# Two-layer mixture-of-experts kernel after an attention layer on one Trainium2 core: transposes of the attention weights from TensorE to VectorE, scores one batch further ahead, and item lists computed along the free dimension

## The chip, the cores and the metric

The kernel runs on one core of a Trainium2 chip. The metric is the device time in microseconds (us) of one execution, the median of three runs. Engines are named as in the profile: PE is TensorE (matrix multiplication), DVE is VectorE, ACT is ScalarE, POOL is GpSimd, SP is SyncE, which here only issues DMAs.

## The reference

Three layers, all in fp32. First an attention in two steps, for 8 batches of 8 heads, with 32 packed queries `p` and 576 positions. Then two mixture-of-experts layers over the 4608 rows, each row to the expert with the largest logit; the second also skips rows.

```python
p_packed = sm_attn(p, k, v)              # 32 queries against 576 keys, per head
out = sm_attn(q, p_packed, p_packed)     # 576 queries against 32 packed rows
x = out.transpose(0, 2, 1, 3).reshape(8 * 576, 512)
# layer 1: e = argmax(x @ w_gate); x = gate * relu(x @ w1[e]) @ w2[e]
# layer 2: rows with x @ w_skip > 0 only:
#          e = argmax(x @ w_gate); x = x + gate * relu(x @ w1[e]) @ w2[e]
```

With the inputs given nearly all rows of a batch choose one expert in the first layer. The few others and the second layer are worked through as lists of items (batch, expert), found while the kernel runs.

## The kernel before

**Loop over batches.** The main loop runs over the 8 batches of the first layer. The main work of batch `b` is `gen_M`: for each half of the 576 columns, `stage1` (8 hidden tiles, line 750, each of 6 matmuls of 128x288) and `stage2` (4 output tiles, line 779, each of 24 matmuls). Every product is made from split operands (a high part and a low part `...l`), three matmuls for one. `stage1` ends in a high half on ACT (`hh`, line 762) and a low half on DVE (`hl`, line 763); `stage2` reads the eight `hh` and `hl` in the order 3, 2, 1, 0, 7, 6, 5, 4.

**What is woven in.** `Weave` goes through the 48 steps of the main work and lets side work (other generators) issue its instructions between them, each at a share of the loop that the `plan` and `sides` give. Side work marked `TE` may only come at every fourth step, so that different kinds of small matmuls stand together in one lump between the large ones. The side work of batch `b` is the attention of the next batches: `gen_S` of batch `b+1` and `b+2` (first softmax), `gen_T` of batch `b+1` (second softmax), `gen_R` (routing), `gen_pre` (weights of the next batch's expert), and the routing of the second layer. The order on each engine comes from this program order and a scheduler at build time. Every engine works through its own queue in order.

**gen_S** makes scores (32 heads' rows, line 384, `s<-kT,pT`), their maxima on DVE (line 426), exponentials on ACT into `a1` (line 438; 128 partitions, 2x576), and the sums. Then PE turns `a1` by 8 transposes of 128x128 (line 455) and one of the tail `tl` (line 459), ACT copies the results from PSUM to `aT` (line 458), and PE multiplies by `v` (lines 468 and 474). The result `pk` is scaled on DVE (line 483), turned on PE (line 488), and gives three small sums on DVE: `kb`, `kw`, `ks` (lines 493 to 501). `gen_T` needs `ks` for a matmul that picks the batch's expert (line 521); it stands in PE's queue right behind the score matmuls of `gen_T`.

**Lists.** `first_item` (end of batch 6) finds the first item of the second layer. `y_list` finds all others while the first item's main work runs (`e_item`, 32 steps of 12 matmuls). Both count flags over partitions by small matmuls with `sel`, `tri` and `ones` (lines 892, 896, 902, 917, 922, 923, 955). `x_flags` counts the left-over rows of the first layer (line 1020). The list `lyB` is read by SP, which then loads the next item's rows and weights.

Of the kernel before, what the change touches and what calls it, by code (L numbers as in the profile page):

```python
# [9 lines left out]
F32 = mybir.dt.float32  # L10
# [11 lines left out]
E = 8  # L22
# [6 lines left out]
XB = 6  # L29
# [89 lines left out]
def attn_moe_kernel(ctx, tc, q, k, v, p, wg, w11, w12, w21, w22, out):  # L119
# [48 lines left out]
    lyA = ct("lyA", [32, 1], I32)  # L168
# [19 lines left out]
    def gen_consts():  # L188
        for t, x in ((sel, 0.0), (valy, 0.0), (GMx, 0.0), (FM, 0.0), (FX, 0.0), (csx, 0.0)):
            nc.gpsimd.memset(t, x)  # L190
        nc.gpsimd.memset(sel[0:1, :], 1.0)
        nc.gpsimd.memset(valy[:, 3:4], 1.0)
# [27 lines left out]
        nc.vector.tensor_copy(valy[:, 0:1], q8[0:64, :])  # L220
        nc.vector.tensor_copy(valy[:, 2:3], m8[0:64, :])
# [16 lines left out]
    lnA = const.tile([64, 1], F32, name="lnA")  # L238
# [72 lines left out]
    def gen_prefix(fc, nch, n):  # L311
# [13 lines left out]
        nc.vector.tensor_copy(pc[:, 0:nch], p0[0:n, 0:nch])  # L325
        return pc
# [80 lines left out]
    def gen_S(b):  # L407
        d = st[b]
# [34 lines left out]
        tl = wk_p.tile([128, 2, 64], F32, name="tl")  # L443
        nc.vector.tensor_copy(tl, a1[:, :, 512:S])
# [6 lines left out]
        aT = wk_p.tile([128, 9, 128], F32, name="aT")  # L451
# [7 lines left out]
        nc.tensor.transpose(ats[2][:, 0:128], tl.rearrange("p x c -> p (x c)"), ident)  # L459
        nc.scalar.copy(out=aT[:, 8, :], in_=ats[2][:, 0:128])  # L460
# [157 lines left out]

    def gen_attn():
        for b in range(1, B):  # L620
            yield from gen_T(b)
            if b + 1 < B:
                if b == 1:
                    with tc.issue_after(hold[-1]):
                        load_all(b + 1)
                else:
# [242 lines left out]
    def y_flags(f2, v, k):  # L869
        nc.vector.tensor_scalar(out=f2[:, 0, :], in0=v, scalar1=float(SMALL), scalar2=None, op0=ALU.is_gt)  # L870
        if k > 1:
            nc.vector.scalar_tensor_tensor(
                out=f2[:, 1, :], in0=v, scalar=0.0, in1=f2[:, 0, :], op0=ALU.is_gt, op1=ALU.subtract
            )

    def first_item():
# [11 lines left out]
        f2 = rt.tile([32, 3, n], F32, name="f2", bufs=1)  # L888
        y_flags(f2, fl.rearrange("p b e -> p (b e)"), 1)
        yield  # L890
        ps = mt("f0")
        nc.tensor.matmul(out=ps[0:n, 0:1], lhsT=f2[:, 0, :], rhs=sel[:, 0:1], start=True, stop=True)
        fc = rt.tile([64, 3], F32, name="yfc", bufs=1)
        nc.vector.tensor_copy(fc[:, 0:1], ps[0:n, 0:1])
        yield
        nc.tensor.matmul(out=ps[0:n, 8:9], lhsT=tri[0:n, 0:n], rhs=fc[:, 0:1], start=True, stop=True)
        nc.vector.scalar_tensor_tensor(
            out=lnA, in0=ps[0:n, 8:9], scalar=1.0, in1=fc[:, 0:1], op0=ALU.is_equal, op1=ALU.mult
        )
        yield  # L900
        l0 = mt("l0")
        nc.tensor.matmul(out=l0[0:32, 0:1], lhsT=valy, rhs=lnA, start=True, stop=True)
        nc.vector.tensor_copy(lyA, l0[0:32, 0:1])
        yield

    def y_list():
# [856 lines left out]
```

## Time and profile before

| | |
|---|---|
| median of 3 runs | 584.71 us (584.62 to 585.27) |
| profiled execution, its own time | 585.04 us |
| its span, first to last instruction | 583.3 us |
| mean granted clock of TensorE | 0.998 |
| PE busy | 573.2 us (98%) |
| DVE busy | 327.9 us (56%) |
| ACT busy | 217.9 us (37%) |
| POOL busy | 132.2 us (23%) |

The span is 1.7 us shorter than the execution's own time. A busy time is the union of an engine's instructions, and matmuls are pipelined: the mean duration of one is longer than the distance between two starts.

### The profile page before, as it was taken

Reading aid. Unit: us, or ns where it says so; the run is one execution under the profiler, and the core shown is the slowest. Engines: PE = TensorE matmul, PEld = TensorE weight load, DVE = VectorE, ACT = ScalarE, POOL = GpSimd, SP = SyncE. Lnnn points to the kernel's source line nnn. Section 1 sums busy time; section 2 is a strip of 40 time slices with the busy share of each in tenths; the row PEclk is TensorE's granted clock in tenths of the full one; section 3 lists DMA queues with packets and bytes.
Section 4 is the critical chain, followed back from the end, with each engine's and each line's share of the span. In section 5 each row is a group of like instructions: output and inputs, shape, how many; then the busy total and the mean of one; then the engine's idle time right before and its main releaser. Section 6 shows DMA issues by size and latency. Waiting matters only on the chain. (4 is left out here: it accounts for less than half of the span.)

```text
span 583.3 us, 14454 instructions
## 1 busy us (share of the span) xinstructions
PE 573.2 (98%) x5798; PEld 532.2 (91%) x5799; DVE 327.9 (56%) x995; ACT 217.9 (37%) x477; POOL 132.2 (23%) x121
## 2 busy tenths in 40 slices
PE   8899999999999999999999999999999999999996
PEld 6489899899999989989989998899999999998796
DVE  3898658566566757646756864346736327162111
ACT  3464542452462353444346234133414325042110
POOL 3051331331240150133133114020301310130031
PEclk9999999999999999999999999999999999999999
DMA  8945978787485767826714616997047583731065
GB/s 338 364 163 202 420 324 318 262 312 269 156 302 167 308 209 238 330 74 261 277 58 187 236 45 223 330 302 265 6 173 255 99 342 93 199 97 70 1 90 86
DMA packets 33806, 123.23 MB, mean 211 GB/s; under 512 B 5424, under 2 KB 15536, under 8 KB 25648
## 3 DMA queue, kind: packets, MB, share of 16 engines
q1 hardware_dynamic: 28304, 116.16, 53.3%
q0 software_dynamic: 3824, 4.70, 6.2%
q10 hardware_dynamic: 1584, 1.18, 0.6%
q8 instruction: 51, 0.84, 0.6%
q14 instruction: 43, 0.35, 0.2%
HBM read 92.77 MB, written 29.26 MB: 209 GB/s over the span
## 5 line engine op out<-in xcount | busy, mean ns | idle before, releaser
L779 PE MATMUL y<-hh,W2h 128*128 128x288 f32 x512 | 154.4, 302 | 0.0
L779 PE MATMUL y<-hl,W2h 128*128 128x288 f32 x512 | 151.2, 295 | 0.0
L779 PE MATMUL y<-hh,W2l 128*128 128x288 f32 x512 | 150.9, 295 | 0.0
L779 PEld LDWEIGHTS y<-hh,W2h 128*128 128x128 f32 x512 | 96.0, 188 | 4.9 <-DVE Q1l L646 2.8
L779 PEld LDWEIGHTS y<-hh,W2l 128*128 128x128 f32 x512 | 96.4, 188 | 0.0
L779 PEld LDWEIGHTS y<-hl,W2h 128*128 128x128 f32 x512 | 96.2, 188 | 0.1
L646 POOL TENSOR_TENSOR W2l<-W2c,W2h 128x1024 fp32r<-128x1024 f32 x28 | 66.7, 2391 | 124.6 <-ACT W2h L644 105.5
L750 PE MATMUL h<-A2h,Q1h 128*128 128x288 f32 x256 | 76.6, 299 | 0.0
L750 PE MATMUL h<-A2h,Q1l 128*128 128x288 f32 x256 | 75.7, 296 | 0.0
L750 PE MATMUL h<-A2l,Q1h 128*128 128x288 f32 x256 | 75.5, 295 | 0.0
L763 DVE SCALAR_TENSOR_TENSOR hl<-h,hh 128x288 fp32r<-128x288 f32 x128 | 56.4, 452 | 29.5 <-ACT hh L762 29.4
L762 ACT ACTIVATE hh<-h 128x288 fp32r<-128x288 f32 x128 | 51.7, 412 | 55.3 <-PE h L750 52.8
L750 PE MATMUL h<-eXh,eW1h 128*128 128x288 f32 x192 | 57.7, 301 | 0.2 <-issue 0.2
L1380 PE MATMUL y<-ihh,iW2h 128*128 128x288 f32 x192 | 56.8, 296 | 0.0
L1380 PE MATMUL y<-ihl,iW2h 128*128 128x288 f32 x192 | 56.6, 295 | 0.0
L1380 PE MATMUL y<-ihh,iW2l 128*128 128x288 f32 x192 | 56.6, 295 | 0.0
L750 PE MATMUL h<-eXl,eW1h 128*128 128x288 f32 x192 | 56.5, 295 | 0.0
L750 PE MATMUL h<-eXh,eW1l 128*128 128x288 f32 x192 | 56.5, 294 | 0.0
L750 PEld LDWEIGHTS h<-A2h,Q1h 128*128 128x128 f32 x256 | 48.0, 187 | 2.1 <-DVE Q1l L646 0.8
L750 PEld LDWEIGHTS h<-A2h,Q1l 128*128 128x128 f32 x256 | 48.1, 188 | 0.2
L750 PEld LDWEIGHTS h<-A2l,Q1h 128*128 128x128 f32 x256 | 48.1, 188 | 0.0
L644 ACT CAST W2h<-W2c 128x1024 fp32r<-128x1024 f32 x30 | 31.6, 1054 | 39.3 <-PE y L779 21.8
(311 smaller groups left out, 937.3 us busy)
## 6 DMA issues: line engine op xcount, KB each, us to landing
eW<-in_w_dram SPq DMA_DIRECT2D x8, 2048.0 KB
W2c<-in_w_dram SPq DMA_DIRECT2D x30, 512.0 KB
v<-in_v_dram SPq DMA_DIRECT2D x7, 1280.0 KB
W1c<-in_w_dram SPq DMA_DIRECT2D x8, 1024.0 KB
y<-in_w_dram SPq DMA_DIRECT2D x8, 1024.0 KB
kT<-in_k_dram SPq DMA_DIRECT2D x7, 1152.0 KB
qT<-in_q_dram SPq DMA_DIRECT2D x7, 1152.0 KB
x2d<-y SPq DMA_DIRECT2D x7, 1152.0 KB
```

Of the source, the lines that this page charges most:

```text
L644: a = nc.scalar.copy(out=hi, in_=x)
L646: z = eng.tensor_tensor(out=lo, in0=x, in1=hi.bitcast(F32), op=ALU.subtract)
L750: m = nc.tensor.matmul(out=ps[:, 0:rh.shape[2]], lhsT=l[:, t, 128 * f:128 * f + 128], rhs=r[:, t, :], start=(n == 0), stop=(n == 3 * kt - 1),)
L762: us[0]["hh"] = nc.scalar.activation(out=hh[:, f, :], in_=ps[:, 0:n_], func=ACTF.Relu).ins
L763: ins = nc.vector.scalar_tensor_tensor(out=hl[:, f, :], in0=ps[:, 0:n_], scalar=0.0, in1=hh[:, f, :].bitcast(F32), op0=ALU.max, op1=ALU.su ...
L779: nc.tensor.matmul(out=ps[:, 0:HALF], lhsT=l[:, f, :], rhs=r[:, f, :], start=(n == 0), stop=(n == 23))
L1380: nc.tensor.matmul(out=ps[:, 0:HALF], lhsT=l[:, f, 128 * t:128 * t + 128], rhs=r[:, f, c], start=(n == 0), stop=(n == 23))
```

## The change

For batches 3 to 7 `a1` is no longer turned by PE. DVE does it in 32x32 blocks: 16 instructions (`gen_Sx`), each from 32 partitions of `a1` to 32 partitions of `aT`, 8 blocks (256 elements per partition) each. The tail keeps its PE transpose. For this, the scores and exponentials (`gen_Sa`) of a batch come one batch earlier, and its `k` and `p` with them; batch 3's scores go into the second half of batch 1 as a new piece of side work. Batches 0 to 2 are as before. `first_item` and `y_list` now hold the 64 flags in the free dimension on 32 partitions: a prefix sum in six DVE additions, a DVE transpose, and one product of two matmuls at the end take the place of the matmuls with `sel`, `tri` and `ones`. `x_count` moves the count of left-over rows into the matmul lump of the prefix, and a `yield TE` joins another small matmul to a later lump. The loads for the item behind the first come 0.03 of a loop later.

```diff
+    def gen_S(b):
+        yield from gen_Sa(b)
+        yield from gen_Sb(b)
...
+    def tail(b):
+        tl = st[b]["tl"] = wk_p.tile([128, 2, 64], F32, name="tl")
+        nc.vector.tensor_copy(tl, st[b]["a1"][:, :, 512:S])
+
+    def gen_Sx(b):
...
+        for h in range(4):
+            for g in range(4):
+                nc.vector.transpose(
+                    out=aT[32 * g:32 * g + 32, 0:8, 32 * h:32 * h + 32].rearrange("p (x j) c -> p x j c", x=2),
+                    in_=a1[32 * h:32 * h + 32, :, 0:512].rearrange("p x (j g c) -> p x j g c", g=4, c=32)[:, :, :, g, :],
+                )
+                if (h, g) == (3, 3):
+                    tail(b)
+                yield
...
-        ats = [mt("at") for _ in range(3)]
-        for x in range(2):
-            for j in range(4):
-                last = nc.tensor.transpose(ats[x][:, 128 * j:128 * j + 128], a1[:, x, 128 * j:128 * j + 128], ident).ins
-            if b == 0 and x == 0:
-                keep(3, last)
-            nc.scalar.copy(out=aT[:, 4 * x:4 * x + 4, :].rearrange("p j c -> p (j c)"), in_=ats[x])
+        if b < AHEAD:
...
+        else:
+            aT = d["aT"]
...
-                    load_all(b + 1)
-                yield from gen_S(b + 1)
+                    if b + 2 < B:
+                        load_k(b + 2)
+                    load_q(b + 1)
+                    load_v(b + 1)
+                    yield from gen_Sb(b + 1)
...
+        for i in range(6):
+            a, z, k = P[i % 2], P[1 - i % 2], 2 ** i
+            nc.vector.tensor_tensor(out=z[:, :, H:], in0=a[:, :, H:], in1=a[:, :, H - k:H + n - k], op=ALU.add)
...
-            nc.tensor.matmul(out=ps[0:n, i:i + 1], lhsT=f2[:, i, :], rhs=sel[:, 0:1], start=True, stop=True)
...
+        for k in range(2):
+            nc.tensor.matmul(out=l0[0:32, 0:2 * w + 3], lhsT=valy[:, k, :], rhs=O[:, k, :], start=(k == 0), stop=(k == 1))
...
+                    if b == 1:
...
+                        s3 = gen_Sa(3)
+                        sides.append((part(s3, 1), 1, 0.3, 0.35))
+                        sides.append((s3, 6, 0.405, 0.5, TE))
+                    sides.append((gen_Sx(b + 2), 17, *((0.55, 0.84) if b == 1 else (0.45, 0.82))))
+                    if b + 3 < B:
+                        s4 = gen_Sa(b + 3)
+                        sides.append((part(s4, 1), 1, 0.6, 0.65))
+                        sides.append((s4, 5, 0.81, 1.0, TE))
...
-        return [(part(ld, 1), 1, 0.37, 0.38), (ld, 1, 0.56, 0.57), (pre(), 8, 0.55, 1.0)]
+        return [(part(ld, 1), 1, 0.37 + z, 0.38 + z), (ld, 1, 0.56, 0.57), (pre(), 8, 0.55 + z, 1.0)]
```

How the instructions stand on an engine is given below in rows of the built program: line, operation, output and inputs, shape, and how many in a row.

DVE in the second half of the first `stage1` of batches 2 to 5, up to the sum `ks` for which PE's line 521 (570 in the changed kernel) waits. Before:

```order
L272 STREAM_TRANSPOSE gT<-GM_76 128x160
L763 SCALAR_TENSOR_TENSOR hl<-h,hh 128x288
L845 SCALAR_TENSOR_TENSOR fT<-gT,once 128x160
L763 SCALAR_TENSOR_TENSOR hl<-h,hh 128x288
L850 TENSOR_REDUCE csB<-fT 128x1
L763 SCALAR_TENSOR_TENSOR hl<-h,hh 128x288 x2
L493 TENSOR_REDUCE kb<-ps 128x4
L497 TENSOR_TENSOR kw<-wgAB,kb 128x32
L501 TENSOR_REDUCE ks<-kw 128x8
```

The same place in the changed kernel; the first of the four `hl` stands just ahead of these rows, and one more transpose `aT<-a` five rows ahead:

```order
L273 STREAM_TRANSPOSE gT<-GM_75 128x160
L818 SCALAR_TENSOR_TENSOR hl<-h,hh 128x288
L484 STREAM_TRANSPOSE aT<-a_3389 32x8x32
L818 SCALAR_TENSOR_TENSOR hl<-h,hh 128x288
L484 STREAM_TRANSPOSE aT<-a_3389 32x8x32
L818 SCALAR_TENSOR_TENSOR hl<-h,hh 128x288
L542 TENSOR_REDUCE kb<-ps 128x4
L484 STREAM_TRANSPOSE aT<-a_3389 32x8x32
L546 TENSOR_TENSOR kw<-wgAB,kb 128x32
L900 SCALAR_TENSOR_TENSOR fT<-gT,once 128x160
L550 TENSOR_REDUCE ks<-kw 128x8
```

Four transposes now stand ahead of `ks`, and `csB` has gone behind it.

DVE in the second half of batch 1, around the eight `hl` of the second `stage1`. Before:

```order
L570 STREAM_TRANSPOSE A_1430<-T_1377 128x288 x2
L646 TENSOR_TENSOR A2l<-A_1430,A2h 128x576
L797 TENSOR_TENSOR y_145<-y,gB 128x288
L763 SCALAR_TENSOR_TENSOR hl<-h,hh 128x288 x8
L646 TENSOR_TENSOR A2l<-A_1430,A2h 128x576
```

In the changed kernel, from behind `A2l` up to the second `hl`; the pattern of one transpose and one `hl` goes on to the eighth `hl`, with two transposes in one place:

```order
L469 TENSOR_SCALAR sm<-sm 128x1
L472 RECIPROCAL rc_1515<-sm 128x1
L852 TENSOR_TENSOR y_144<-y,gB 128x288
L469 TENSOR_SCALAR sm<-sm 128x1
L484 STREAM_TRANSPOSE aT<-a_1605 32x8x32
L472 RECIPROCAL rc_1515<-sm 128x1
L484 STREAM_TRANSPOSE aT<-a_1605 32x8x32
L818 SCALAR_TENSOR_TENSOR hl<-h,hh 128x288
L484 STREAM_TRANSPOSE aT<-a_1605 32x8x32
L818 SCALAR_TENSOR_TENSOR hl<-h,hh 128x288
```

Four maxima (line 448) and two small instructions (line 455) of batch 3's scores also stand ahead, between the transposes of `A` and `A2l`; ten transposes in all stand ahead of the eighth `hl`.

PE in `y_list`, in the first item of the second layer; `h` are main matmuls. Before (the matmul of line 955 follows nine main matmuls behind these rows):

```order
L917 MATMUL f_7259<-sel,f_7255 64x1 x3
L750 MATMUL h<-eXh,eW1h 128x288
L750 MATMUL h<-eXl,eW1h 128x288
L750 MATMUL h<-eXh,eW1l 128x288
L922 MATMUL f_7259<-yfc,tri 64x2
L923 MATMUL f_7259<-yfc,ones 64x1
```

The changed kernel has one lump there, 36 main matmuls later than line 955 stood before, counted from the item's start:

```order
L805 MATMUL h<-eXl,eW1h 128x288
L805 MATMUL h<-eXh,eW1l 128x288
L1017 MATMUL l_7369<-Oy,valy 32x133 x2
L805 MATMUL h<-eXh,eW1h 128x288
L805 MATMUL h<-eXl,eW1h 128x288
```

Three lumps (917, 922 with 923, and 955) have become one, with two products of half the depth.

## Rows read from the trace of the kernel before

**Rows 1.** The page's busy times, and the longest wait of PE: total, times, longest.

```profile
PE 573.2 (98%) x5798; PEld 532.2 (91%) x5799; DVE 327.9 (56%) x995; ACT 217.9 (37%) x477; POOL 132.2 (23%) x121
...
PE keep L347 <- DVE fl L884: 1.7, 1, 1.7
```

**Rows 2.** PE's timeline, main matmuls in batch 1: start, duration, instruction.

```profile
100.03 0.30 PE L750 MATMUL h<-A2h,Q1l 128*128 128x288 f32 x1
...
104.96 0.29 PE L779 MATMUL y<-hh,W2h 128*128 128x288 f32 x1
```

**Rows 3.** PE's timeline, the transposes of batch 3's weights, in batch 2.

```profile
123.99 1.04 PE L455 MATMUL at<-ident,a 128*128 128x128 f32 x8
124.87 0.27 PE L459 MATMUL at<-ident,tl 128*128 128x128 f32 x1
```

**Rows 4.** Busy times over the loops of batches 2 to 5 (four windows).

```profile
sum 183.00, PE 182.86 PEld 171.64 DVE 113.75 ACT 77.71 POOL 47.10; mean PE 45.72 PEld 42.91 DVE 28.44 ACT 19.43 POOL 11.78
```

**Rows 5.** DVE's groups by shape: transposes, two copies, maxima; busy, mean ns.

```profile
L570 DVE STREAM_TRANSPOSE A<-T 128x288 f32<-128x288 f32 x32 | 13.5, 459 | 7.6 <-POOL T L566 7.6
L426 DVE TENSOR_REDUCE mx<-s 128x1 f32<-128x288 f32 x32 | 13.1, 447 | 6.5 <-PE s L384 6.5
L281 DVE STREAM_TRANSPOSE LT<-L 128x160 f32<-128x160 f32 x16 | 5.5, 346 | 10.4 <-PE L L825 10.4
L1261 DVE COPY xro<-xT 128x256 f32<-128x256 f32 x1 | 0.4, 424 | 0.9 <-PE xT L1260 0.9
L1100 DVE COPY xh<-hT 128x256 f32<-128x256 f32 x1 | 0.4, 415 | 0.0
L281 DVE STREAM_TRANSPOSE LT<-L 32x32 f32<-32x32 f32 x1 | 0.2, 205 | 0.9 <-PE L L1118 0.9
```

**Rows 6.** Timeline of DVE up to `ks`, and PE's matmul on it, batch 3.

```profile
177.00 0.34 DVE L272 STREAM_TRANSPOSE gT<-GM 128x160 f32<-128x160 f32 x1
177.27 0.16 DVE L266 TENSOR_TENSOR GM<-oh,g 128x40 f32<-128x40 f32 x1
...
178.81 0.30 DVE L850 TENSOR_REDUCE csB<-fT 128x1 f32<-128x160 f32 x1
179.03 0.81 DVE L763 SCALAR_TENSOR_TENSOR hl<-h,hh 128x288 fp32r<-128x288 f32 x2
179.76 0.28 DVE L493 TENSOR_REDUCE kb<-ps 128x4 f32<-128x128 f32 x1
180.31 0.21 DVE L501 TENSOR_REDUCE ks<-kw 128x8 f32<-128x32 f32 x1
...
181.57 0.17 PE L521 MATMUL s<-ks,ones 64*32 64x8 f32 x1
```

**Rows 7.** Timeline in batch 0, where PE waited for `ks`.

```profile
16.31 0.21 DVE L501 TENSOR_REDUCE ks<-kw 128x8 f32<-128x32 f32 x1
...
16.66 0.20 PE L517 MATMUL s<-ks,ones 128*32 128x8 f32 x2 [0.16 <-DVE ks L501]
```

**Rows 8.** PE's timeline around the lumps of lines 892 and 917.

```profile
354.54 0.30 PE L779 MATMUL y<-hh,W2l 128*128 128x288 f32 x1
...
355.21 0.29 PE L779 MATMUL y<-hl,W2h 128*128 128x288 f32 x1
...
422.90 0.29 PE L750 MATMUL h<-eXh,eW1l 128*128 128x288 f32 x1
...
423.79 0.29 PE L750 MATMUL h<-eXl,eW1h 128*128 128x288 f32 x1
```

**Rows 9.** DVE's timeline, first and last of eight `hl`, batch 1.

```profile
100.07 0.46 DVE L763 SCALAR_TENSOR_TENSOR hl<-h,hh 128x288 fp32r<-128x288 f32 x1 [0.84 <-ACT hh L762]
...
105.61 0.46 DVE L763 SCALAR_TENSOR_TENSOR hl<-h,hh 128x288 fp32r<-128x288 f32 x1 [0.34 <-ACT hh L762]
```

**Rows 10.** Timeline: the second item's last split on DVE, its first matmul.

```profile
447.08 1.21 DVE L646 TENSOR_TENSOR eW1l<-eW,eW1h 128x1024 fp32r<-128x1024 f32 x1
...
460.10 0.29 PE L750 MATMUL h<-eXh,eW1h 128*128 128x288 f32 x1
```

More of the change, by code (lines that the diff above doesn't have):

```diff
@@ L219, in gen_consts @@
         nc.vector.tensor_copy(valx[:, :, 2], m8[0:NXP, :].to_broadcast([NXP, 2 * B]))
-        nc.vector.tensor_copy(valy[:, 0:1], q8[0:64, :])
-        nc.vector.tensor_copy(valy[:, 2:3], m8[0:64, :])
+        for i in range(2):
+            nc.vector.tensor_scalar(
+                out=valy[:, i, 0:1], in0=q8[0:32, :], scalar1=4.0 * i, scalar2=None, op0=ALU.add
+            )
+            nc.vector.tensor_copy(valy[:, i, 2:3], m8[0:32, :])
         yield
@@ L309, in store_gm, with x_count, gen_prefix @@
             )
-    def gen_prefix(fc, nch, n):
+    def x_count(p0):
+        nc.tensor.matmul(out=p0[0:32, 64:64 + 2 * B], lhsT=ones[0:NXP, 0:32], rhs=X["FL"], start=True, stop=True)
+        nc.vector.tensor_reduce(
+            out=X["cnt"], in_=p0[0:32, 64:64 + 2 * B].rearrange("p (b z) -> p b z", z=2), op=ALU.add, axis=AX.X
+        )
+        cx = X["cx"]
+        for i, (a, z) in enumerate(((0, XB), (XB, B))):
+            nc.vector.tensor_reduce(out=cx[:, i:i + 1], in_=X["cnt"][:, a:z], op=ALU.add, axis=AX.X)
+        nc.vector.tensor_scalar(
+            out=cx[:, 2:3], in0=cx[:, 0:1], scalar1=-1.0, scalar2=0.0, op0=ALU.add, op1=ALU.max
+        )
+        nc.vector.tensor_tensor(out=cx[:, 2:3], in0=cx[:, 2:3], in1=cx[:, 1:2], op=ALU.add)
+        nc.vector.tensor_copy(cxi, cx)
+        nc.vector.tensor_scalar(out=cx[:, 2:3], in0=cx[:, 2:3], scalar1=0.0, scalar2=None, op0=ALU.is_equal)
+    def gen_prefix(fc, nch, n, more=None):
         if nch > 1:
@@ L325, in gen_prefix @@
         nc.vector.tensor_copy(pc[:, 0:nch], p0[0:n, 0:nch])
+        if more is not None:
+            more(p0)
         return pc
@@ L617, in attn_moe_kernel @@
     hold, fence = [], []
+    AHEAD = 3
     def gen_attn():
@@ L887, in first_item @@
         )
-        f2 = rt.tile([32, 3, n], F32, name="f2", bufs=1)
-        y_flags(f2, fl.rearrange("p b e -> p (b e)"), 1)
+        f = fl.rearrange("p b e -> p (b e)")
+        nc.vector.tensor_scalar(out=f, in0=f, scalar1=float(SMALL), scalar2=None, op0=ALU.is_gt)
         yield
[L891 to L894, printed above, removed]
@@ L895, in first_item @@
-        yield
-        nc.tensor.matmul(out=ps[0:n, 8:9], lhsT=tri[0:n, 0:n], rhs=fc[:, 0:1], start=True, stop=True)
-        nc.vector.scalar_tensor_tensor(
-            out=lnA, in0=ps[0:n, 8:9], scalar=1.0, in1=fc[:, 0:1], op0=ALU.is_equal, op1=ALU.mult
+        key = X["h"][0:32, 0:n]
+        nc.vector.scalar_tensor_tensor(
+            out=key, in0=iot[0:32, 0:n], scalar=-float(n + 1), in1=f, op0=ALU.add, op1=ALU.mult
+        )
+        m = rt.tile([32, 1], F32, name="ym", bufs=1)
+        nc.vector.tensor_reduce(out=m, in_=key, op=ALU.min, axis=AX.X)
@@ new lines, in y_list @@
+        nc.vector.tensor_scalar(out=f0, in0=v, scalar1=float(SMALL), scalar2=None, op0=ALU.is_gt)
+        nc.vector.scalar_tensor_tensor(out=f1, in0=v, scalar=0.0, in1=f0, op0=ALU.is_gt, op1=ALU.subtract)
+        nc.vector.tensor_scalar(out=f64, in0=v, scalar1=64.0, scalar2=None, op0=ALU.is_gt)
+        nc.vector.tensor_tensor(out=f0, in0=f0, in1=lnA, op=ALU.subtract)
+        yield
+        H = n // 2
+        P = [rt.tile([32, 2, H + n], F32, name=f"yp{i}", bufs=1) for i in range(2)]
+        for p in P:
+            nc.vector.memset(p[:, :, 0:H], 0.0)
@@ L953, in y_list @@
+        nc.vector.tensor_copy(O[:, :, 2 * w:2 * w + 3], T[:, 3:6, :].rearrange("p q k -> p k q"))
         yield
         l0 = mt("l0")
-        nc.tensor.matmul(out=l0[0:32, 0:2 * w + 3], lhsT=valy, rhs=O, start=True, stop=True)
+        for k in range(2):
+            nc.tensor.matmul(out=l0[0:32, 0:2 * w + 3], lhsT=valy[:, k, :], rhs=O[:, k, :], start=(k == 0), stop=(k == 1))
         nc.vector.tensor_copy(lyB[:, 0:2 * w], l0[0:32, 0:2 * w])
@@ L1019, in x_flags, with x_prep @@
         )
-        nc.tensor.matmul(out=f0[0:32, 64:64 + 2 * B], lhsT=ones[0:NXP, 0:32], rhs=FL, start=True, stop=True)
-        nc.vector.tensor_reduce(
-            out=X["cnt"], in_=f0[0:32, 64:64 + 2 * B].rearrange("p (b z) -> p b z", z=2), op=ALU.add, axis=AX.X
-        )
-    def x_prep(X, b0, nb):
+    def x_prep(X, b0, nb, more=None):
         b0, nb = 2 * b0, 2 * nb
@@ L1487, in attn_moe_kernel @@
             W.add(g, 1, 0.85, 1.0)
-            W.add(first_item(), 4, 0.75, 0.9)
+            first = first_item()
+            W.add(part(first, 2), 2, 0.75, 0.85)
+            W.add(first, 4, 0.92, 1.0)
             W.add(expect("nox"), 1, 0.92, 0.92)
```

170 lines of the change are left out of this document (89 added, 81 removed).

## The prediction

> **What bounds the kernel now.** I read the page's busy times first: PE is busy for 573.2 of 583.3 us, DVE for 327.9, ACT for 217.9 and POOL for 132.2. The chain that ended last names only the final instructions, so I took PE's list of waits next: its longest wait is 1.7 us, at the start [rows 1]. From about 26 us to the end PE works without a pause, one main matmul every 4.93 / 37 = 0.133 us (the two rows are 37 matmuls apart) [rows 2]. So an instruction taken from PE's queue there gives back the time that it holds PE, as long as PE then waits for nobody. Two things are to be weighed: what the removed matmuls hold, and which of PE's waits, all zero today, become real because DVE gets more to do. In the loops of batches 2 to 5 DVE is busy for a mean of 28.4 of 45.7 us [rows 4], so it has room on average. What counts is the room at the places where PE waits for DVE.
>
> **What PE loses.** The 8 transposes of a batch hold PE from 123.99 to 124.87, that is 0.88 us, 0.11 each [rows 3]. They go for five batches (3 to 7): 5 x 0.88 = **4.4 us**. The tail's transpose stays, and with it the cost of entering and leaving the lump, so no more than that is gained here.
>
> The small list matmuls cost more by breaking the stream than by themselves. Around line 892 two main matmuls start 0.67 us apart with one between them, against 2 x 0.133: the lump costs 0.40. Around line 917 (three products) it is 0.89 - 0.27 = 0.62 [rows 8]. Of `first_item` three lumps go (892, 896, 902), all single products: 3 x 0.40 = 1.2. Of `y_list` two go, line 917 at 0.62 and 922 with 923, two products, which I put between the two rows at 0.5: 1.1. The lump of line 955 becomes two products in place of one; a pass over 128 columns in fp32 took 0.11 [rows 3], and I count two more passes of 133: 0.2 lost. Line 1020 joins the lump of the prefix: 0.40 less some 0.1 for its own passes, 0.3. Line 1046 joins the lump of the next batch's weights, which I price at half a lump, 0.2. Against that, the scores of batch 3 leave a lump that stays (at the end of a loop, batch 7's place in batch 5) for one of their own in batch 1: half a lump lost, 0.2. Together 1.2 + 1.1 - 0.2 + 0.3 + 0.2 - 0.2 = **2.4 us**, and PE's queue is shorter by 6.8 us in all. The bounds of the lumps: each of the five that go between 0.3 and 0.62, so 1.9 to 3.2 in place of 2.4.
>
> **What a transpose on DVE costs.** No row shows one of 32 partitions by 256 elements with gaps between its blocks. The nearest are 128x160 at 346 ns and 128x288 at 459 ns [rows 5]; by the line through them 256 elements take 0.43 us. Instructions of DVE overlap by some 0.07 (the row behind a 0.34 us transpose starts 0.27 later [rows 6]), so each holds the queue for **0.36 us**, and 16 of them 5.8 us per batch: DVE's mean goes from 28.4 to 34.2 of 45.7. That the blocks are scattered I price at nothing: a copy that rearranges 256 columns took 424 ns and a plain one 415 [rows 5]. The lower end is 0.27, that of the 160 elements. The upper end: the row of one 32x32 block took 205 ns; if every block paid that, 8 would take 1.6 us. The 128x160 row has 5 block columns and took 0.346, not 5 x 0.2, which is why I go by the line.
>
> The Trainium skill, VectorE: DVE Perf Modes, section Rules for kernel authors, speaks against this step: a 128x128 transpose belongs on TensorE if a PSUM destination will do, and VectorE only turns 32x32 blocks. Counted as engine time it is right here: 0.88 us of PE become 5.8 of DVE, and if DVE's time were paid one for one, the sum would be 5 x (5.8 - 0.88) = 25 us slower (an estimate from the rows above). It is not paid so as long as DVE's time is spare.
>
> **Where PE could now wait for DVE.** First, `ks`, in batches 2 to 5. DVE ends it at 180.31 + 0.21 = 180.52 and PE takes it at 181.57 [rows 6]: 1.05 us to spare. DVE runs through this stretch without a gap. Four transposes now stand ahead: 4 x 0.36 = 1.44. `csB` goes behind `ks`, 0.22 back (178.81 to 179.03); and from `kb` to `ks` took 0.55 for two small instructions that wait for each other [rows 6], of which the fourth transpose fills some 0.1. So `ks` comes 1.1 later. In batch 0, where PE did wait, it started 0.14 after the end of `ks` [rows 7]. 1.1 + 0.14 - 1.05 leaves a wait of about 0.1 to 0.2: **0.6 us** for four batches. This turns on the price: at 0.46 per transpose it is 0.6 each, at 0.27 nothing. What stands behind `ks` on DVE has a gap of its own ahead of it today and waits for PE.
>
> Second, the eight `hl` of the second `stage1` in batch 1. Today they start from 100.07 to 105.61 [rows 9], 0.79 apart, because ACT delivers at that pace; the last ends at 106.07. `stage2` starts at 104.96 [rows 2] and wants that one with its 14th matmul, 1.73 later, at 106.7: 0.6 spare. Now four maxima (0.45 each by their row [rows 5], 0.37 with the overlap), six small instructions of some 0.15 and two transposes come ahead of the first `hl`: 1.5 + 0.9 + 0.7 = 3.1, less the idle 0.84 [rows 9], so it is 2.3 late. Between them stand 8 transposes in 7 gaps: an `hl` (0.37) and 1.14 x 0.36 fill 0.78 of 0.79, so the lateness stays. PE itself comes later by the scores' lump, some 1.3. That leaves 2.3 - 1.3 - 0.6 = **0.4 us** of wait, once; 0 to 1.5.
>
> Covered are: ACT, which loses two copies per batch; the `k` loads, which only come a batch earlier, while `q` and `v` come later by as much, each ahead of its use by most of a loop; and the later list `lyB`. Its matmul stands 36 main matmuls (4.8 us) later, so the next item's loads and splits come that much later at most; its last split ended at 447.08 + 1.21 = 448.3 and PE wanted it at 460.10 [rows 10], 11.8 to spare. `y_list`'s own DVE instructions, about 30 of some 0.1 to 0.2 us, stand between `hl` that have 1.6 us each. Without that cover they would cost some 4 us.
>
> **The sum.** -6.8 + 0.6 + 0.4 = -5.8 us. The profiled execution took 585.04 with a span of 583.3, so it becomes 579.2; the median of the runs stands 0.33 lower, and 584.71 - 5.8 = **578.9 us**.
>
> **The rivals.**
> - *Waits at `ks` and `hl` are larger.* The transposes cost what the 128x288 row says without overlap, 0.46. Then `ks` waits 0.6 in four batches (2.4) and the ten transposes ahead of the last `hl` add 1.0 to 0.4. -6.8 + 2.4 + 1.4 = -3.0: 581.7 us. For it: `ks` has no slack left by my own count. Against it: back-to-back rows overlap.
> - *No wait at all*, because the transposes hold 0.27 to 0.33 or DVE's order closes gaps that I left: -6.8, and lumps at their upper bound another -0.4: 577.6 us.
> - *Slower: each 32x32 block pays a start of its own.* In the four waits at `ks` and the one at `hl` stand 4 x 4 + 10 = 26 transposes, so every 0.1 us more per transpose costs 2.6 us; from 0.36 + 5.8 / 26 = 0.58 us on the kernel is slower than before. At 1.6 us (8 blocks at 0.205) it would be 26 x 1.24 - 5.8 = +26: 611 us. Against it: the 128x160 row; for it: no row has this shape. VectorE becoming the bound, as the skill's rule would have it, is this same case.
> - *No change:* a wait in batch 1 eats the gain, if batch 3's keys or the order of `a1` (one buffer, written a batch earlier) hold up PE for 5 us or more. The DMA engines are busy in that loop, but the keys are issued at the same place as before, and the transposes that free `a1` end before the next exponentials.
>
> **How the numbers follow.** My forecast 0.6; larger waits 0.2; no wait 0.1; slower 0.05; no change 0.05. 0.2% (1.2 us) is about what a measurement of this kernel can tell from no change; the first three are all faster by more than that: 0.9. The forecast's own range is 577.9 to 580.2 (transposes at 0.33 to 0.42, lumps at their bounds); the whole range takes in both neighbours, 577.3 to 581.9, and leaves out 0.1 above and little below.
>
> **What the changed profile would show.** Transposes `aT` at 0.43 us each in DVE's groups; PE's group of line 455 at 24 in place of 64; PE busy some 6 us less, with waits of 0.1 to 0.2 at the matmul on `ks` and under 1 us at `stage2` of batch 1. I would be wrong if a transpose takes over 0.5 us, if PE shows a wait that I have not named (the tail's transpose, the first matmuls of a batch, the start of the second item), or if the lumps of the lists cost PE less than their distances say.

## The result, and the profile after

The changed kernel takes **588.62 us** (median of 5 runs, 586.99 to 591.51) against 584.71 (584.42 to 585.27): a ratio of 1.0069 [1.0051, 1.0087], slower by 0.7%. The forecast was 578.9. The profiled execution is the longest of the five: 591.51, span 589.9, mean granted clock 0.992. The fastest, 586.99, has 0.999, and between them the time rises as the clock falls, so a part of the loss is one that not every execution pays. Even the fastest is 2.3 us above the median before.

The page's busy times, and PE's list of waits behind the start (total, times, longest), to set against [rows 1]:

```profile
PE 571.4 (97%) x5744; PEld 529.3 (90%) x5745; DVE 372.5 (63%) x1093; ACT 211.1 (36%) x467; POOL 132.0 (22%) x119
```

```profile
PE mp L916 <- DVE mw L910: 2.5, 1, 2.5
PE y L834 <- DVE hl L818: 1.9, 1, 1.9
PE s L570 <- DVE ks L550: 1.4, 4, 0.4
PE h L805 <- DVE ero L1447: 0.6, 1, 0.6
```

Before, PE had no wait over 0.2 us behind 26 us. Now it has two large ones, one on the last `hl` of batch 1 (which I had put at 0.4) and one on `mw` in the first item of the second layer (which I had not named). Behind each of them the clock falls. PE's windows around the two (start:end, length, busy and matmuls, granted clock, DMA share, GB/s):

```profile
108.00:110.00 2.00, 1.94 (x15) 1.00 1.03 418
110.00:112.00 2.00, 0.29 (x3) 1.00 1.06 441
112.00:114.00 2.00, 1.86 (x11) 0.82 0.99 419
114.00:116.00 2.00, 2.00 (x10) 0.50 0.73 299
116.00:118.00 2.00, 2.00 (x14) 0.83 0.09 37
...
418.00:420.00 2.00, 0.16 (x2) 1.00 0.03 8
420.00:422.00 2.00, 1.39 (x7) 0.62 0.00 0
422.00:424.00 2.00, 2.00 (x10) 0.53 0.00 0
424.00:426.00 2.00, 2.00 (x18) 1.00 0.00 0
```

At a granted clock of 0.50, the lower level (1.2 of 2.4 GHz), ten main matmuls go through in a window that otherwise holds 17 or 18. The trace's record of the clock gives each of the two stretches 3.41 us at half speed, so each costs 3.41 / 2 = 1.7 us. That also explains most of PE's busy time: it fell by 1.8 where I had some 6, and 3.4 of it is there only because matmuls took twice as long.

Where the 6.6 us of span came from shows when the distances between the first main matmuls of successive loops (differences of their starts in the timelines, us) are set side by side. The last three columns are experiments, told below:

| loop | before | after | attention alone | lists alone | turned from batch 4 on |
|---|---|---|---|---|---|
| batch 1 | 47.12 | 52.68 | 51.50 | 47.11 | 48.43 |
| batch 2 | 47.46 | 46.99 | 46.99 | 47.45 | 48.41 |
| batch 3 | 47.13 | 46.95 | 47.32 | 47.12 | 46.95 |
| batch 4 | 47.13 | 46.95 | 46.95 | 47.12 | 46.95 |
| batch 5 | 47.13 | 46.03 | 45.98 | 47.12 | 46.07 |
| batch 6 | 50.16 | 48.06 | 49.29 | 49.25 | 48.33 |
| batch 7 | 45.36 | 45.38 | 45.36 | 45.92 | 45.36 |
| first item to second | 54.94 | 58.65 | 54.61 | 53.50 | 57.31 |

The start is 1.5 us later as well, but the first main matmul comes at 26.8 to 28.8 us in the profiles here, with no order by kernel, so this is not shown to be the change's doing. Batch 1 loses 5.6: about 1.3 for the scores that moved into it (the last column, which has them without the wait, shows 1.3), 1.85 for the wait, 1.7 for the clock, and some 0.7 of small gaps. The first item loses 3.7: 2.45 for the wait, 1.7 for the clock and 0.64 for a wait at its end, less the 1.4 that the lists give there; 0.3 is left open. The other loops give back 4.0 together: 2.1 in batch 6, of which the lists alone give 0.9, 1.1 in batch 5, which has no later batch's scores to make any more, and 0.5 in batch 2. What the turning itself gives shows in batches 3 and 4, where nothing else differs: **0.18** each, not the 0.73 forecast (0.88 less a wait of 0.15).

### The profile page after: what moved, and what is told of

Read it like the earlier page. It is cut to its first block, busy times and chain, and to the rows that moved or that the text cites. A ratio compares the mean times of both kernels' runs of the same rounds, so it can differ in the third digit from the quotient of the medians.

```text
span 589.9 us, 14415 instructions
## 1 busy us (share of the span) xinstructions
PE 571.4 (97%) x5744; PEld 529.3 (90%) x5745; DVE 372.5 (63%) x1093; ACT 211.1 (36%) x467; POOL 132.0 (22%) x119
## 5 line engine op out<-in xcount | busy, mean ns | idle before, releaser
L818 DVE SCALAR_TENSOR_TENSOR hl<-h,hh 128x288 fp32r<-128x288 f32 x128 | 54.5, 450 | 17.1 <-ACT hh L817 16.6
L852 DVE TENSOR_TENSOR y<-y,gB 128x288 f32<-128x288 f32 x48 | 21.7, 453 | 43.4 <-PE y L834 36.6
```

The source lines that it names most:

```text
L818: ins = nc.vector.scalar_tensor_tensor(out=hl[:, f, :], in0=ps[:, 0:n_], scalar=0.0, in1=hh[:, f, :].bitcast(F32), op0=ALU.max, op1=ALU.su ...
L852: nc.vector.tensor_tensor(out=y1[:, t, cols], in0=ps[:, 0:HALF], in1=d["gB"][:, cols], op=ALU.mult)
```

## The experiments

The runs before these kernels, on the same chips, had medians of 584.96 to 585.16. Each ratio below is against those.

**1 and 2. Each part alone.** The first kernel takes only the changes to `gen_S`, the transposes and the plan of the attention; the second only those to `first_item`, `y_list` and `x_count`.

> The changed attention alone: turning by VectorE in batches 3 to 7, scores a batch ahead; the lists of second-layer items stay as they were. Theory A (batch 1 asks more of VectorE than it has time for, and PE's wait there brings a stretch at the 1.2 GHz clock): the wait for hl of about 1.9 us and the half-clock stretch of about 3.4 us (1.7 us lost) in batch 1 stay, the four ks waits of 0.36 us stay, 5 x 0.88 us of transposes are gone; the kernel ends 0 to 2 us above the kernel before, and the later half-clock stretch near 420 us is absent, since the mass matmul stands where it stood. Rival (the attention part is a gain as predicted, and the lists lose it): 2 to 4 us below the kernel before.

> The changed lists alone; attention is turned on PE as before. Theory B (the time lost in item 0 is VectorE waiting about 2.9 us behind its branch for code, and then sharing its time with a GpSimd split, and whether the code is there depends on where the branch and its target stand in VectorE's instructions): here the branch and its target stand elsewhere than in the changed kernel, as far into the program as in the kernel before, so the gap behind the branch is about 0.6 us, the mass matmul does not wait over 0.5 us, and the kernel is 1.5 to 2.5 us faster than before. Rival (the lists themselves are late, since the mass matmul now stands 6 us earlier in PE's order): the wait of about 2.5 us and the half-clock stretch are here too, and the kernel is 1.5 to 3 us slower than before.

Attention alone: 586.13 (584.89 to 588.41), ratio 1.0021 [1.0008, 1.0034]. Lists alone: 583.03 (582.77 to 583.57), 0.9967 [0.9954, 0.998], which beats both kernels. So the attention is slower by itself by 1.1 us, the lists are worth 2.0, and both together should give about 0.9 less; they give 3.9 more. Some 4.8 us arise only where both are. Attention alone has the wait on `hl` in its trace too, at the same length, 1.85, and not the half clock behind it that I had expected (its list of waits, and PE's windows there):

```profile
PE y L816 <- DVE hl L800: 2.4, 2, 1.9
```

```profile
110.00:112.00 2.00, 0.17 (x1) 1.00 0.99 419
112.00:114.00 2.00, 2.00 (x16) 1.00 1.00 419
```

**3. The transposes of batch 1 spread over more of the loop.**

```diff
-sides.append((gen_Sx(b + 2), 17, *((0.55, 0.84) if b == 1 else (0.45, 0.82))))
+sides.append((gen_Sx(b + 2), 17, *((0.55, 1.0) if b == 1 else (0.45, 0.82))))
```

> The changed kernel with batch 1's 17 turning steps over 0.55 to 1.0 of the batch instead of 0.55 to 0.84, so that one comes every 1.2 us and not every 0.8 us. Theory A: a step of 0.44 us and an hl of 0.46 us no longer have to fit into the 0.80 us that PE gives a pair of them, the wait for hl of 1.9 us and the half-clock stretch in batch 1 are gone, 2.5 to 3.6 us less than the changed kernel. Rival (the backlog comes from the scores of batches 3 and 4, which both fall into batch 1, not from the turning): the wait stays over 1 us, and the time is within 1 us of the changed kernel.

589.77 (586.98 to 591.86), 1.0068 [1.0052, 1.0083]: nothing gained, and PE's wait on `hl` is again 1.9. The edit did not do what I meant. The share of the loop sets where the program issues them, but DVE still has a transpose between every two `hl`, so the order of the build decided it. It neither supports nor refutes the cause.

**4. Forty small fills on DVE,** 40 memsets of one element, to move everything behind them to another place in DVE's instruction stream. In the changed kernel DVE comes out of a branch of the program (line 1645) into the first item and does nothing for 2.83 us; before, it was 0.52, and attention alone has the long gap too (2.82). They are written into batch 6, but the build put them at the program's start: they run from 1.7 to 13.0 us, not from 370 to 395 as I had expected. They still stand ahead of the branch.

```diff
+def pads():
+    for _ in range(8):
+        for _ in range(5):
+            nc.vector.memset(junk, 0.0)
+        yield
-W = Weave(gen_M(b, (1,)), NM // 2, [])
+W = Weave(gen_M(b, (1,)), NM // 2, [(pads(), 8, 0.02, 0.3)])
```

> The changed kernel with 40 one-element fills on VectorE between 370 and 395 us, where it is half idle; they do nothing but move every later instruction of VectorE by 40 places. Theory B: the gap behind VectorE's branch before item 0 falls from 2.9 to about 0.6 us, the mass matmul waits under 0.5 us, and the half-clock stretch behind it is gone, 3.5 to 4.5 us less than the changed kernel. Rival (the lists are late of themselves, or GpSimd's split holds VectorE): the wait of 2.5 us stays, and the time is that of the changed kernel or up to 1 us more.

586.57 (585.39 to 590.91), 1.0028 [1.0009, 1.0047]: 2.0 less than the changed kernel, where 3.5 to 4.5 was expected. The profiled execution, 590.76, is one of the two slowest of nine. In it the gap behind the branch is 0.52 again, as expected from the place alone, but PE's wait on `mw` stays:

```profile
PE mp L916 <- DVE mw L910: 2.9, 1, 2.9
```

So the late branch is not all of it. DVE's and GpSimd's timelines of this kernel show the second half:

```profile
414.70 2.42 DVE L900 SCALAR_TENSOR_TENSOR fT<-xgT,once 128x160 f32<-128x160 f32 x1 [0.80 <-DVE xgT L273]
...
417.51 1.84 DVE L910 TENSOR_TENSOR mw<-csB,E 128x16 f32<-128x16 f32 x1
...
414.54 4.78 POOL L701 TENSOR_TENSOR iW2l<-eW,iW2h 128x1024 fp32r<-128x1024 f32 x2 [27.29 <-ACT iW2h L699]
```

`fT` and `mw`, 0.33 and 0.17 us before, take 2.42 and 1.84 while GpSimd makes its two splits of the item's second weights, and both have two operands in SBUF, as the splits have.

**5 and 6. The two stalls taken away one at a time.** The first kernel turns only batches 4 to 7 on DVE, so that batch 1 has no transposes. The second adds 12 tiny copies on ACT in batch 6 to the 40 fills, to put ACT's branch too back where it was slow (2.74 us idle, as in the kernel before), so that ACT casts later and GpSimd starts later.

```diff
-AHEAD = 3
+AHEAD = 4
...
-sides.append((gen_Sx(b + 2), 17, *((0.55, 0.84) if b == 1 else (0.45, 0.82))))
+if b + 2 >= AHEAD:
+    sides.append((gen_Sx(b + 2), 17, 0.45, 0.82))
```

```diff
+def apads():
+    for _ in range(12):
+        nc.scalar.copy(out=jnk[:, 1:2], in_=X["FL"][0:1, 0:1])
+        yield
+W.add(apads(), 12, 0.3, 0.6)
```

> The changed kernel with batch 3 turned on PE again (no VectorE transposes in batch 1; the scores of batch 3 stay where the change put them). Theory A (16 VectorE transposes between the hl steps of batch 1's second half make the last hl late): the 1.9 us wait for hl and the half-clock stretch of 1.7 us behind it are gone, 0.9 us of PE transposes come back, so 2 to 3.5 us less than the changed kernel. Rival (the exponentials of batch 3's scores, which now fall into batch 1 too and hold ScalarE for 2 us just as its first hh are due, make hl late): a wait of over 1 us stays.

> As the run with 40 fills on VectorE, and 12 one-element copies on ScalarE in batch 6 besides, which do nothing but put ScalarE's branch before item 0 where the kernel before has it among ScalarE's instructions. Theory B2 (ScalarE finds its code at once in the changed kernel, 0.36 us instead of 2.49, so GpSimd's split of iW2l starts before VectorE's chain to the mass weights and holds it up): ScalarE's gap is 2.4 to 2.8 us again, GpSimd starts at least 1.5 us after VectorE's branch is through, fT and mw take 0.33 and 0.17 us, the mass matmul does not wait and the half-clock stretch behind it is gone, so 3.5 to 4.5 us less than with the fills alone. Rival (VectorE's chain is late for another reason): mw ends over 2 us after PE is there, as with the fills alone.

From batch 4 on: 586.32 (584.68 to 588.50), 1.0023 [1.0009, 1.0037], 2.3 less than the changed kernel. The wait on `hl` is 0.2 and batch 1 has no half clock, so it is the transposes that make that wait, not the exponentials of batch 3's scores, which stay where they were; the wait on `mw` stays, with half clock behind it. Its waits:

```profile
PE mp L916 <- DVE mw L910: 2.0, 1, 2.0
...
PE y L834 <- DVE hl L818: 0.2, 1, 0.2
```

With ACT late: 586.08 (583.35 to 587.39), 1.0014 [1.0001, 1.0027], 2.5 less than the changed kernel, but only 0.5 less than the fills alone, where 3.5 to 4.5 was expected; by their times the two kernels can't be told apart. In the profiled execution it is the other way round from run 5: the wait on `hl` and the half clock behind it stay, and the list of waits has no `mp` any more. Its timeline shows why:

```profile
414.37 2.94 ACT L699 CAST iW2h<-eW 128x1024 fp32r<-128x1024 f32 x3 [2.74 <-DVE xgT L273]
...
416.50 5.78 POOL L701 TENSOR_TENSOR iW2l<-eW,iW2h 128x1024 fp32r<-128x1024 f32 x2 [28.62 <-DMA gm2d<-xgT]
...
414.31 0.33 DVE L900 SCALAR_TENSOR_TENSOR fT<-xgT,once 128x160 f32<-128x160 f32 x1 [0.80 <-DVE xgT L273]
...
415.02 0.18 DVE L910 TENSOR_TENSOR mw<-csB,E 128x16 f32<-128x16 f32 x1
```

ACT is idle for 2.74 us ahead of its casts, 2.4 more than with the fills alone, GpSimd starts 2 us later, and DVE's two instructions are through before it. A later engine took a wait away; what that is worth in time this pair of runs doesn't show.

**7 and 8. GpSimd's splits given to DVE,** the second with 5's edit and 56 fills as well.

```diff
-split(..., nc.gpsimd if t % 2 else nc.vector)
+split(..., nc.gpsimd if t % 2 and "f0" not in d else nc.vector)
```

> The changed kernel with item 0's two GpSimd splits of iW2l made by VectorE; nothing else differs, and VectorE's gap of 2.83 us behind the branch stays. Theory B2: fT takes 0.33 us instead of 2.44, mw is ready about 2.1 us earlier, the wait of the mass matmul falls from 2.5 to about 0.4 us, the half-clock stretch behind it is gone: 2 to 4 us less than the changed kernel. Rival (the gap alone makes the wait): over 2 us of wait stay and the time is that of the changed kernel.

> Batch 3 on PE, item 0's GpSimd splits on VectorE, and 56 fills on VectorE at the program's start so that its branch stands where its code was ready at once: all three places taken away together. If A and B2 hold: no wait over 0.5 us behind the start, no half-clock stretch before the end, the lists' 2.0 us and four batches' 0.88 us of transposes are gained, 1.4 us of ks waits are paid: 580.5 to 582 us, faster than the kernel before and than the lists alone. Rival (what is taken away comes back elsewhere, at the next late step): 583 us or more.

590.49 (589.28 to 591.26), 1.0091 [1.0078, 1.0105], and 584.02 (582.29 to 588.31), 0.9992 [0.9974, 1.0011]. The flag is no longer set where the edit asks for it, so GpSimd made its two splits in both. The first is a second copy of the changed kernel and tells nothing of the cause. It does tell how firm the median is: the two copies lie 1.9 apart, and against this one, which ran together with runs 5 and 6, those are faster by 4.2 and 4.4, not by 2.3 and 2.5. The second has batch 1 cured and the DVE branch short; `mw` took 1.90 beside GpSimd but came just in time, so PE's matmul did not wait. Expected for it was 580.5 to 582.

**9 and 10. The same, now reaching GpSimd.** The engine is passed in from the caller, where the flag is still set. The second kernel adds 5's edit and the 56 fills, everything that helped.

```diff
-def gen_ew2(d):
+def gen_ew2(d, other):
...
-split(..., nc.gpsimd if t % 2 else nc.vector)
+split(..., other if t % 2 else nc.vector)
...
-[(gen_ew2(d), 4, 0.0, 0.25)]
+[(gen_ew2(d, nc.vector if "f0" in d else nc.gpsimd), 4, 0.0, 0.25)]
```

> The changed kernel with item 0's two GpSimd splits of iW2l now truly made by VectorE (in the run before this the edit did not reach them); VectorE's gap of 2.83 us behind its branch stays. Theory B2 (two things hold the mass matmul up one behind the other, the missing code and then GpSimd's splits): fT takes 0.33 us instead of 2.44, mw is ready about 2.1 us earlier, the wait of the mass matmul falls from 2.5 us to about 0.4, no half-clock stretch follows: 3 to 4 us less than the changed kernel. Rival (the gap alone makes the wait): over 2 us of wait stay.

> Batch 3 turned on PE, item 0's GpSimd splits made by VectorE, and 56 fills at the start so that VectorE's code is ready behind the branch. If A and B2 are the whole of the loss: no wait of PE over 0.9 us behind the first 26 us, no half-clock stretch before the last 5 us, and a time between 582.0 and 583.5 us: about what the lists alone give (583.0 us), since four batches of turning save 0.88 us each but pay about 0.4 us of waits for ks and 0.3 us of late hl in the batches that hold VectorE's transposes. Rival (the attention part is a clear gain once batch 1 is out of it): 581.5 us or less.

Without GpSimd: 585.95 (584.83 to 588.04), 1.0020 [1.0009, 1.0031], 2.7 less than the changed kernel. DVE's timeline and PE's waits:

```profile
414.53 0.32 DVE L900 SCALAR_TENSOR_TENSOR fT<-xgT,once 128x160 f32<-128x160 f32 x1 [3.10 <-issue]
...
415.25 0.17 DVE L910 TENSOR_TENSOR mw<-csB,E 128x16 f32<-128x16 f32 x1
```

```profile
PE mp L916 <- DVE mw L910: 0.3, 1, 0.3
```

Expected was 3 to 4. The late branch is still there (3.10 of idle time), but it alone makes PE wait 0.3. In run 4 it was the other half alone, GpSimd's splits with the short branch, and the wait was 2.9. So it is GpSimd's splits beside DVE's two instructions that make the long wait. All of it together: 583.67 (582.57 to 584.90), 0.9978 [0.9968, 0.9988], with no wait of PE over 0.9 behind the start. Expected was 582.0 to 583.5. That beats the kernel before, but not the lists alone (583.03, and the two intervals overlap): with both stalls gone, turning on DVE is worth nothing that these runs can show.

**11 and 12. A wait of known length in the kernel with the lists alone,** made by 6 or 4 idle transposes (0.37 us each) ahead of `csB` in the first item, with GpSimd out of the way.

```diff
+if b == B - 1:
+    for _ in range(6):          # 4 in the other
+        held = nc.vector.transpose(out=junk, in_=fT).ins
+with tc.issue_after(held) if held is not None else nullcontext():
     nc.vector.tensor_reduce(out=csB[:, b:b + 1], in_=fT, op=ALU.add, axis=AX.X)
```

> The lists alone (583.0 us), GpSimd's splits of item 0 on VectorE, and six idle transposes of 0.36 us each in VectorE's chain ahead of the mass weights, which do nothing but make mw late; with one split of 1.22 us that falls in between, mw comes about 2.2 us after PE asks for it. Theory C (a wait of PE of about 2 us costs itself and 1.7 us more, since PE's clock then stands at 1.2 GHz for 3.4 us): 3 to 4.5 us more than the lists alone, a granted clock of 0.5 for 3.4 us behind the wait in the profile. Rival (the half-clock stretches were not the waits' doing): 1.5 to 2.5 us more.

> The same with four idle transposes, ahead of both splits: mw comes 0.2 to 0.7 us after PE asks for it. Theory C: a wait this short brings no half-clock stretch, so 0 to 0.8 us more than the lists alone, and no stretch at a granted clock of 0.5 before the last 5 us. Rival: a stretch here too, or over 1.5 us more.

Six: 585.77 (584.82 to 587.43), 2.74 above the lists alone, between the expected 3 to 4.5 and the rival's 1.5 to 2.5; PE's wait on `mw` is 2.52. Four: 583.89 (582.61 to 585.06), 0.86 above; the wait is 0.57. The two differ by 1.9 us in time and 1.95 in the wait, so a wait of PE there is paid about one for one. (The lists alone with GpSimd's splits on DVE and no idle transposes were not run.) Behind the wait of 2.5 the profiled execution shows full clock (its list of waits, and PE's windows):

```profile
PE mp L885 <- DVE mw L879: 2.5, 1, 2.5
...
416.00:418.00 2.00, 0.00 (x0) 1.00 0.02 8
418.00:420.00 2.00, 1.62 (x13) 1.00 0.02 4
```

My theory that such a wait always brings a half-clock stretch falls with this. The 12 runs of this kernel fall into two groups, 584.8 to 585.4 at clocks of 0.997 to 1.000 and 586.1 to 587.4 at 0.994 to 0.997, their means 1.7 apart. That fits a stretch in some executions, but only one of them was profiled, and its one stretch stands at 25 us, behind a wait of 2.2 on a weight load.

## Why the prediction was wrong

**What the turning takes from PE was right.** The group of PE's transposes has 24 instructions in place of 64, and a transpose on DVE takes 0.436 us (I had 0.43). That the blocks are scattered costs nothing beyond the line through the two plain shapes, and the rival on the other side in its own form, a start for every block, is out.

**What a transpose holds was not.** "Instructions of DVE overlap by some 0.07 ... so each holds the queue for **0.36 us**" is the step that failed for the attention. DVE's timeline of the changed kernel, first six of them back to back in batch 2, then between the `hl` of batch 1:

```profile
141.61 2.68 DVE L484 STREAM_TRANSPOSE aT<-a 32x256 f32<-32x256 f32 x6
...
104.67 0.46 DVE L818 SCALAR_TENSOR_TENSOR hl<-h,hh 128x288 fp32r<-128x288 f32 x1
105.16 0.44 DVE L484 STREAM_TRANSPOSE aT<-a 32x256 f32<-32x256 f32 x1
105.61 0.46 DVE L818 SCALAR_TENSOR_TENSOR hl<-h,hh 128x288 fp32r<-128x288 f32 x1
106.08 0.44 DVE L484 STREAM_TRANSPOSE aT<-a 32x256 f32<-32x256 f32 x1
...
111.63 0.46 DVE L818 SCALAR_TENSOR_TENSOR hl<-h,hh 128x288 fp32r<-128x288 f32 x1
```

Six take 2.68, 0.447 each: no overlap at all. The overlap of the rows that I went by is still there in this trace, and one `aT` in each batch has it too:

```profile
103.59 0.21 DVE L469 TENSOR_SCALAR sm<-sm 128x1 f32<-128x1 f32 x1 [0.19 <-ACT a L460]
103.72 0.42 DVE L484 STREAM_TRANSPOSE aT<-a 32x256 f32<-32x256 f32 x1
104.08 0.11 DVE L472 RECIPROCAL rc<-sm 128x1 f32<-128x1 f32 x1
104.20 0.43 DVE L484 STREAM_TRANSPOSE aT<-a 32x256 f32<-32x256 f32 x1
...
153.12 1.63 DVE L619 STREAM_TRANSPOSE A<-T 128x288 f32<-128x288 f32 x4
```

Four transposes over all 128 partitions take 1.63, 0.408 each where one alone takes 0.456. The first `aT` of a batch, which by the diff reads and writes from partition 0 on like its neighbours, starts 0.08 before the instruction ahead of it ends, and the next one starts 0.06 before it ends, in all five batches. The other 15 of a batch read or write from another group of 32 partitions than the instruction ahead of them, and none of these 75 overlaps with a neighbour: there are at least 0.013 us between them. So the rows that gave me 0.07 differ from this instruction in the partitions that they start at.

An `hl` and a transpose take 0.94, and ACT brings the next `hh` after 0.79 [rows 9]. "An `hl` (0.37) and 1.14 x 0.36 fill 0.78 of 0.79, so the lateness stays" is therefore wrong: the lateness grows. The last `hl` starts at 111.63, the first at 104.67, 6.96 for seven steps where it was 5.54; and the first is 3.1 late against the start of the batch, not 2.3. Together the last one is 4.5 late. PE itself is 2.1 later at the matmul on that one (I had 1.3) and had 0.6 to spare: 4.5 - 2.1 - 0.6 leaves 1.8, and the wait is 1.85, not 0.4. The same price is in the waits on `ks`: 0.3 to 0.4 in four batches, 1.4 in all, not 0.6 (the rival had 2.4). That is my first rival's mechanism (0.46 without overlap), to which I gave 0.2. Its own sum, 581.7, was still far off, for what comes next.

**A wait not named: late `hl` in every batch.** With the 16 transposes of a batch, DVE has no gap over 0.12 us in batch 2 from 131 us up to the `hl` of the second `stage1`; before, it had gaps of 1.57, 1.71 and 1.01 us there. So it comes to these eight `hl` late, does them in one run, and `stage2` takes its first one late. The timeline, batch 2 of the changed kernel:

```profile
157.43 3.01 DVE L818 SCALAR_TENSOR_TENSOR hl<-h,hh 128x288 fp32r<-128x288 f32 x8
159.04 0.19 PEld L834 LDWEIGHTS y<-hl,W2h 128*128 128x128 f32 x1 [0.28 <-DVE hl L818]
```

PE's first two matmuls of that `stage2` take 0.58 in place of 0.27 us, 0.31 lost in a batch. So of the 0.88 that the transposes held PE in batches 3 and 4, 0.3 to 0.4 goes into the wait on `ks`, 0.31 into this one, and 0.18 is left. "As long as PE then waits for nobody" was the condition that I wrote and worked out at two places; it had to be worked out at every DVE result that PE takes behind a transpose.

**The lists were right by themselves:** 2.4 forecast, 2.0 measured alone: by the table 0.9 in batch 6 and 1.4 in the first item, less 0.6 in batch 7. (The lower bound of that term was added up wrongly: five lumps at 0.3 in place of 2.3 give 1.6, not 1.9; and its upper bound, 3.2, is 0.8 above the 2.4, not the 0.4 that the rival without waits takes.) What I did not do is to carry the edit to its end: the small matmul on `mw` moves forward in PE's order. Before, DVE ended `mw` 8 us ahead of PE's asking; with the lists alone, by the starts, 1.4 ahead:

```profile
413.27 0.17 DVE L873 TENSOR_TENSOR mw<-csB,E 128x16 f32<-128x16 f32 x1
...
414.69 0.23 PE L879 MATMUL mp<-mw,ones 128*32 128x16 f32 x2
```

That is what was left to spare, and the attention, which adds instructions to DVE and takes some from ACT, spent it. The same instructions before:

```profile
412.02 2.94 ACT L644 CAST iW2h<-eW 128x1024 fp32r<-128x1024 f32 x3 [2.74 <-DVE xgT L272]
...
414.15 5.79 POOL L646 TENSOR_TENSOR iW2l<-eW,iW2h 128x1024 fp32r<-128x1024 f32 x2 [28.59 <-DMA gm2d<-xgT]
...
411.96 0.33 DVE L845 SCALAR_TENSOR_TENSOR fT<-xgT,once 128x160 f32<-128x160 f32 x1 [0.80 <-DVE xgT L272]
...
412.67 0.17 DVE L855 TENSOR_TENSOR mw<-csB,E 128x16 f32<-128x16 f32 x1
...
421.17 0.23 PE L861 MATMUL mp<-mw,ones 128*32 128x16 f32 x2
```

In the changed kernel:

```profile
412.95 2.94 ACT L699 CAST iW2h<-eW 128x1024 fp32r<-128x1024 f32 x3 [0.39 <-issue]
...
415.08 4.72 POOL L701 TENSOR_TENSOR iW2l<-eW,iW2h 128x1024 fp32r<-128x1024 f32 x2 [26.49 <-PE h L805]
...
417.55 2.44 DVE L900 SCALAR_TENSOR_TENSOR fT<-xgT,once 128x160 f32<-128x160 f32 x1 [3.13 <-issue]
...
420.38 0.18 DVE L910 TENSOR_TENSOR mw<-csB,E 128x16 f32<-128x16 f32 x1
...
420.61 0.29 PE L916 MATMUL mp<-mw,ones 128*32 128x16 f32 x2 [2.45 <-DVE mw L910]
```

DVE comes out of the branch 2.3 us later than before, ACT 2.3 earlier (0.39 in place of 2.74), so GpSimd's splits now stand where `fT` does, and `fT` ends just behind the second split (419.99 and 419.80). Attention alone has the late branch and `mw` at 1.90 beside GpSimd, but no wait, since its matmul on `mw` stands 4 us behind; lists alone have the early matmul, a short branch and a late ACT. This is the interaction, a wait of 2.45 in the profile with 1.7 of half clock behind it, where the medians have 4.8. Runs 6 and 9 show its cause from both sides in their traces: with GpSimd later the wait is gone, and without its splits it is 0.3.

**The clock was not in the sum.** A forecast that puts a PE wait at its length alone leaves out up to 1.7 us behind it. In the profiled execution two such stretches make 3.4 of the 6.6 us.

**What was missed, added up.** The forecast was a span 5.8 shorter, the profiled execution has one 6.6 longer. Of these 12.4 us, the wait on `ks` makes 0.8 more than I had, the one on the last `hl` 1.45, the late first `hl` of four batches 1.2, the wait on `mw` 2.45, the one ahead of the second item 0.64, the clock 3.4 and the late start 1.5. That is 11.4; the lists' 0.4 and the 0.7 of batch 1 about make up the rest.

**Open.** Why attention alone shows no stretch behind the same wait on `hl`; the wait of 0.6 to 1.0 us ahead of the second item, which is there in the changed kernel and in runs 3, 4, 6, 7 and 8, and not in 1, 2, 5, 9 and 10; some 0.7 us of batch 1. A kernel in which batch 1's transposes stand behind the last `hl` was not run.

## What to carry to other kernels

Work that goes from a saturated engine to one with "room on average" is paid at every place where the saturated engine takes that engine's results: list all of them, and take the moved instruction at its full duration unless rows of the same instruction, on the same partitions, show overlap. When a small matmul moves forward in the saturated engine's queue, work out the slack of its whole chain anew, and count a possible half-clock stretch with every wait of two microseconds. Two parts of a change that each have slack can spend the same slack: try them apart, and keep the one that pays (here the lists, 583.03).

## What the runs showed of the hardware

- **Two engines on one path to SBUF.** In the changed kernel `fT` beside GpSimd's splits takes 2.44 us in place of 0.33 and ends 0.19 behind the second split; without GpSimd it takes 0.32, behind the same late branch. `hl`, with one operand in PSUM, was beside GpSimd's splits 24 times there and never took over 0.46. The Trainium skill, SBUF — State Buffer, section SBUF: two separate sides, says that a VectorE instruction with two SBUF inputs and a GpSimd instruction that reads SBUF lock each other out for a whole instruction; the trace agrees, with those numbers.
- **A branch has a price that depends on its place.** DVE's first instruction behind the same branch comes after 0.52 us in the kernel before, in lists alone and with 40 or 56 fills, and after 2.8 to 3.0 with the attention and no fills; ACT's comes after 0.4 or 2.5 to 2.7. 40 instructions more ahead of it on DVE turn 2.8 into 0.52, 12 on ACT turn 0.4 into 2.5. That it is the loading of instructions is argued, not shown: the Trainium skill, Runtime: NRT & Kernel Launch, section Instruction fetch mechanics, has it that a taken branch stalls where its target is not in the loaded pages. The traces have 8 KB packets of an instruction queue about 1 us behind the branch, but with the long gap (at 415.59, behind 414.55) and the short one (at 412.45, behind 411.29) alike, so they don't show that the gap is a load.
- **Half clock behind short waits.** Stretches of 3.41 us at a granted clock of 0.50 followed waits of PE of 1.85 to 2.9 us in seven of the profiles here, and did not follow waits of 1.85 to 2.6 in four places (attention alone, runs 9 and 11, and the start of run 12). What decides between the two was not found.
- **Two instructions of DVE in a row.** They overlapped by 0.06 to 0.08 us where both start at partition 0, as the first `aT` of a batch and its neighbours do, and not at all where the `aT` reads or writes from another group of 32 partitions (75 of 75 in the changed kernel).
